# Where a weight conversion stands in a fused attention and two-MLP kernel, and which engines do it

## The chip, the cores and the metric

One core of a Trainium2 chip runs the whole program. The metric is the device time of one launch in microseconds (us), the median of several executions.

## What is computed

Windowed attention over 4 x 8 heads of 576 positions, a gated MLP with RMS norm, and a second MLP, all in single precision:

```python
scores = where(0 <= i - j < 64, q @ k.T / 8, -1e9)      # 4 batches, 8 heads, 576 x 64
x  = softmax(scores) @ v                                # 2304 tokens x 512
xn = x / sqrt(mean(x * x) + 1e-6) * rms_g
y  = (silu(xn @ w_gate) * (xn @ w_val)) @ w_out         # 512 -> 1536 -> 512
h  = y @ w_in                                           # 512 -> 2048
out = (h * sigmoid(1.702 * h)) @ w_out2                 # 2048 -> 512
```

The five weight matrices arrive as 64-bit floats, q, k and v as 32-bit floats.

## The kernel before

Every product is done in two parts: an operand is split into a rounded high part and the rest, and three of the four part products are summed. Tokens come in six blocks of 384, feature columns in chunks of 128.

The first half of the gated MLP (`for j in range(NB)`, blocks j = 0 to 5) runs beside the attention of the next block: for each chunk f, `proj` makes the gate and the value in PSUM tiles `psg` and `psv`, and `emit_O` adds the product with `w_out`. At the border of two blocks the next x is scaled (`rms_sum`, `rms_spread`, with a power on GpSimd at L439) and split into `xh` and `xl` (L462 to L466).

The second half (`for sb in range(NSB)`, `for p in range(NP1)`: nine pairs, called pair 0 to 8 here) takes two blocks and two chunks at a time by a scheme of seven products in place of eight. `chain(wg, ...)` makes the four gates and `chain(wv, ...)` the four values. A chain runs seven products of six matmuls into two PSUM tiles, `psa` and `psb`; between them ScalarE copies `psa` out (`snap`, L677) and VectorE adds `psb` to the copy (`plus`, L681). The product after next may not start until its tile has been read. `take` hands each result on: `gated` applies Silu (L853), `valued` multiplies and splits (L863 to L865). `fill` puts the matmuls of `half_groups` of the pair before between the products. TensorE's order is pinned to the program's from block 1 on. On the other engines the compiler orders the instructions by a simulated timeline in which the program's order is the priority, and it lets a ready instruction of low priority run where the engine looks idle. The third part (h chunks, f = 0 to 7 for three pairs of blocks) is built of the same chains.

A weight is turned from 64-bit to 32-bit floats in the kernel, 34 pairs of chunks in `w_order`, called c0 to c33 here. `w_step` does one of them and the second step of the one before it. The two ScalarE instructions (L201 scales the high words, L202 the low words) are kept behind `hold[0]`, the latest gate. VectorE then shifts the high words (L203), puts the sign bit back (L204) and adds the low words as integers (L207). `w_half` starts the next call: `w_products` (for gate, value and `w_in` chunks from c9 on) makes four block differences (L149 to L152), rounds seven blocks on ScalarE (`whi`, L157), makes the rest on VectorE (`wlo`, L158), and stores both to DRAM (L160, L161), from where `t_load` brings them back for each pair. For other chunks L175 and L176 do the same without differences. `w_load` issues the next raw weights on SP (L138). Tiles of tag "st" (raw words and converted words `m`) have 3 buffers, those of tag "w" 11.

c0 to c8 are converted in block 0, c9 to c17 in blocks 1 to 5, c18 to c25 (the `w_in` chunks) in the second half, where each pair of chunks calls `w_step(n_wi)` before its first chain:

```python
                if last:
                    nxo, left = x_first(raws)
                w_step(n_wi)
                a4 = {}
                ...
                chain(wg, xo, lambda i: groups[i - 2]() if i >= 2 else None, gated, nothing)
                ...
                groups = half_groups(sb, p, g, wo)
                wg, wv, wo = nwg, nwv, nwo
```

c26 to c33 (the last matrix) follow at the end of the second half and in the first eight chunks of the third part.

Of the kernel before, what the change touches and what calls it, by code (L numbers as in the profile page):

```python
# [8 lines left out]
F32 = mybir.dt.float32  # L9
F32R = mybir.dt.float32r  # L10
I32 = mybir.dt.int32
U32 = mybir.dt.uint32
AF = mybir.ActivationFunctionType
ALU = mybir.AluOpType
# [8 lines left out]
def window_attention__gated_mlp__mlp_kernel(  # L23
# [13 lines left out]
    nc = tc.nc  # L37
# [53 lines left out]
    def on_pe(op, *args, **kw):  # L91
        ins = op(*args, **kw)  # L92
        if pinned[0]:
            tc.keep_in_program_order(ins)
        return ins
# [16 lines left out]
    n_wh = len(w_order)  # L112
# [4 lines left out]
    n_wi = len(w_order)  # L117
    w_order += [(("p", p), ("p", p + NP2)) for p in range(NP2)]
    n_w = len(w_order)
    w_next = [0, 0]  # L120
# [20 lines left out]
    def after(ins):  # L141
        return tc.issue_after(ins) if ins is not None else nullcontext()
# [3 lines left out]
    def w_products(key, m):  # L146
        b11, b21, b12, b22 = (m[:, i * 256:(i + 1) * 256] for i in range(4))
        t = mt[0][:, 1, :].bitcast(F32).rearrange("p (b c) -> p b c", c=256)
        nc.vector.tensor_tensor(t[:, 0, :], b12, b11, ALU.subtract)  # L149
        nc.vector.tensor_tensor(t[:, 1, :], b22, t[:, 0, :], ALU.subtract)  # L150
        nc.vector.tensor_tensor(t[:, 2, :], b22, b12, ALU.subtract)
        nc.vector.tensor_tensor(t[:, 3, :], b21, t[:, 1, :], ALU.subtract)  # L152
        hi = wp.tile([128, 7, 256], F32R, tag="w", name="whi")
        lo = wp.tile([128, 7, 256], F32R, tag="w", name="wlo")
        for dst, src in ((slice(0, 2), m[:, 0:512]), (slice(2, 3), m[:, 768:1024]), (slice(3, 7), t)):
            src = src if src is t else src.rearrange("p (b c) -> p b c", c=256)
            nc.scalar.copy(hi[:, dst, :], src)  # L157
            nc.vector.tensor_tensor(lo[:, dst, :], src, hi[:, dst, :].bitcast(F32), ALU.subtract)  # L158
        d = dram.tile([128, 2, 7, 256], F32, name="w%s_%d" % key, tag="w%s_%d" % key)
        nc.sync.dma_start(out=d[:, 0], in_=hi.bitcast(F32))  # L160
        nc.sync.dma_start(out=d[:, 1], in_=lo.bitcast(F32))  # L161
        wd[key] = d
# [3 lines left out]
    def w_half():  # L166
        if not half:
            return
        pair, w24 = half.pop()
        kind, p = pair[0]  # L170
        paired = kind == pair[1][0] and p + 1 != pair[1][1]
        if paired and kind in "gvh":
            return w_products(pair[0], w24.bitcast(F32))
        w = wp.tile([128, 2, 1024], F32R, tag="w", name="w")
        nc.scalar.copy(w[:, 0, :], w24.bitcast(F32))  # L175
        nc.vector.tensor_tensor(w[:, 1, :], w24.bitcast(F32), w[:, 0, :].bitcast(F32), ALU.subtract)  # L176
        if paired:
            d = dram.tile([128, 2, 1024], F32, name=f"w{kind}_{p}", tag=f"w{kind}_{p}")
            nc.sync.dma_start(out=d, in_=w.bitcast(F32))
            wd[kind, p] = d  # L180
            weights[kind, p] = w
            return
        for e, key in enumerate(pair):
            weights[key] = w[:, :, e * 512:(e + 1) * 512]

    def w_step(limit):
        w_half()
        if w_next[1] >= min(limit, n_w):
            return
        w_load(w_next[1] + 1)  # L190
        pair = w_order[w_next[1]]
        w_next[1] += 1
        st = staged.pop(0).rearrange("p e (f two) -> p (e f) two", two=2)
        lo, hi = st[:, :, 0], st[:, :, 1]
        if w_next[1] <= n_wh:
            m = wp.tile([128, 1024], I32, tag="w", name="m")
        else:
            mt[0] = stp.tile([128, 2, 1024], I32, tag="st", name="m")
            m = mt[0][:, 0, :]
        with after(hold[0]):  # L200
            nc.scalar.mul(hi.bitcast(F32), hi.bitcast(F32), 2.0 ** -112)  # L201
            nc.scalar.activation(lo, lo.bitcast(U32), AF.Copy, scale=2.0 ** -29)  # L202
        nc.vector.tensor_scalar(m.bitcast(U32), hi.bitcast(U32), 3, None, ALU.logical_shift_left)  # L203
        nc.vector.scalar_tensor_tensor(  # L204
            m.bitcast(U32), hi.bitcast(U32), 0x80000000, m.bitcast(U32), ALU.bitwise_and, ALU.bitwise_or
        )
        nc.vector.tensor_tensor(m, m, lo, ALU.add)  # L207
        half.append((pair, m))
        w_load(w_next[1] + 2)

# [313 lines left out]
    for i in range(m0):  # L524
        m = m0 + i
# [15 lines left out]
    for m in range(2 * m0, N_ATT):  # L541
        b, i = divmod(m, m0)
        t, n = score_at[m - 2 * m0], score_at[m - 2 * m0 + 1] - score_at[m - 2 * m0]
# [13 lines left out]
    if True:  # L557
# [246 lines left out]
        def half_groups(sb, p, g, wo):  # L804
            if p == 0:
                banks = [(acc_p, f"acc{c}") for c in range(4)] + [(atp, "att")] * 2
                accs = [pool.tile([128, 512], F32, tag=tag, name="acc") for pool, tag in banks]
                spots[sb] = [(accs[c], accs[4 + c // 2][:, (c % 2) * 256:(c % 2 + 1) * 256]) for c in range(KC)]
            todo = [(e, c, pi, k) for e in (1, 0) for c in range(KC) for pi in range(3) for k in range(2)]

            def group(lo):
                for e, c, pi, k in todo[lo:lo + 12]:
                    first = p == 0 and e == 1 and pi == 0
                    shared = k == 1 and c % 2 == 1
                    on_pe(
                        nc.tensor.matmul,
                        spots[sb][c][k],
                        wo[:, (0, 1, 0)[pi], e * 512 + c * 128:e * 512 + (c + 1) * 128],
                        g[e][:, (0, 0, 1)[pi], slice(*PIECES[k])],
                        start=first and not shared,  # L820
                        stop=(p == NP1 - 1 and e == 0 and pi == 2),
                        skip_group_check=(k == 1),
                    )
                if p == NP1 - 1 and lo == 36:
                    for c in range(KC):
                        part = osp.tile([128, 2 * TB], F32, tag="os", name="part")
                        nc.sync.dma_start(out=part, in_=osd[sb][:, c, :])
                        for k in range(2):
                            sl = part[:, slice(*PIECES[k])]
                            nc.vector.tensor_tensor(sl, sl, spots[sb][c][k], ALU.add)  # L830
                        nc.sync.dma_start(out=x2d[sb][:, c, :], in_=part)

            return [lambda lo=lo: group(lo) for lo in (0, 12, 24, 36)]

        spots = {}
        for sb in range(NSB):
            last_sb = sb + 1 == NSB
            for p in range(NP1):
                last = p + 1 == NP1
                more = not (last and last_sb)  # L840
                nxt = 0 if last else p + 1
                if more:
                    nwg = t_load(("g", FH + nxt))
                if p == 1:
                    raws = x_raws((lambda e: x2d[0][:, :, e * TB:(e + 1) * TB]) if last_sb else (lambda e: xd[2 * sb + 2 + e]))
                if last:
                    nxo, left = x_first(raws)
                w_step(n_wi)
                a4 = {}

                def gated(q, c):
                    a4[q] = small("a" if q in (0, 3) else "ah")
                    hold[0] = nc.scalar.activation(a4[q], c, AF.Silu).ins  # L853

                chain(wg, xo, lambda i: groups[i - 2]() if i >= 2 else None, gated, nothing)
                if more:
                    nwv, nwo = t_load(("v", FH + nxt)), o_load(("o", FH + nxt))
                g = [xp.tile([128, 2, 2 * TB], F32R, tag="x", name="g") for _ in range(2)]

                def valued(q, c):  # L860
                    e, t = q % 2, q // 2
                    sl = slice(t * TB, (t + 1) * TB)
                    nc.vector.tensor_tensor(a4[q], a4[q], c, ALU.mult)  # L863
                    nc.scalar.copy(g[e][:, 0, sl], a4[q])
                    nc.vector.tensor_tensor(g[e][:, 1, sl], a4[q], g[e][:, 0, sl].bitcast(F32), ALU.subtract)  # L865

                chain(
                    wv, xo, lambda i: groups[i]() if i >= 2 else None, valued,
                    (lambda i: x_next(nxo, left)) if last else nothing,
                )  # L870
                groups = half_groups(sb, p, g, wo)
                wg, wv, wo = nwg, nwv, nwo
            xo = nxo

# [104 lines left out]
```

## Time and profile before

| | us |
|---|---|
| median of 3 runs | 983.26 (982.88 to 983.51) |
| the profiled execution, whole | 981.57 |
| its span on the core | 979.8 |
| TensorE busy in the span | 937.7 |
| VectorE / ScalarE / GpSimd busy | 571.8 / 495.0 / 12.2 |

The profile shows one execution. A row of a timeline gives the start in us from the start of the span, the duration, the engine, the line, the operation with the tiles written and read, and in brackets how long the engine stood idle before and what ended that. A line of groups gives busy time and mean duration. The median of the runs is 1.69 us above the profiled execution.

### The profile page before, as it was taken

How to read it: one execution, taken by the hardware profiler on the slowest of the kernel's cores; microseconds unless marked ns; L12 is line 12 of the kernel's file. 1: busy time of each engine (PE TensorE's matmuls, PEld its weight loads, DVE VectorE, ACT ScalarE, POOL GpSimd, SP SyncE). 2: the span in 40 equal slices, each digit the busy share in tenths (PEclk: the TensorE clock that was granted, in tenths of full speed). 3: DMA queues.
4: the chain of work that ended last, by engine and by line, in shares of the span. 5: the costliest groups of instructions: out<-in, count | busy, mean ns of one | idle time of the engine just before them, and what ended most of it. 6: DMA issues, size and time to landing. Idle time of an engine off the chain costs nothing.

```text
span 979.8 us, 15502 instructions
## 1 busy us (share of the span) xinstructions
PE 937.7 (96%) x5966; PEld 859.7 (88%) x5966; DVE 571.8 (58%) x1207; ACT 495.0 (51%) x1054; POOL 12.2 (1%) x39
## 2 busy tenths in 40 slices
PE   8889999999999897999999989999999999999998
PEld 7789898989989897988988979888888888888887
DVE  5898578577776875677777676645452223422222
ACT  7786566556564344464464365545543333523332
POOL 2000000000000000000000000000000000000000
PEclk9899899999999899999999999999999999999999
DMA  9956376746655589899999898776583535554301
GB/s 223 255 161 175 109 194 179 218 121 194 193 162 186 187 329 412 325 398 385 359 371 352 337 382 316 264 269 246 193 315 139 233 135 220 209 210 172 151 1 65
DMA packets 136074, 228.95 MB, mean 234 GB/s; under 512 B 79936, under 2 KB 106560, under 8 KB 131392
## 3 DMA queue, kind: packets, MB, share of 16 engines
q1 hardware_dynamic: 135472, 227.96, 66.8%
q8 instruction: 47, 0.77, 0.3%
q14 instruction: 27, 0.22, 0.1%
q10 hardware_dynamic: 528, 0.00, 0.0%
HBM read 171.84 MB, written 56.10 MB: 233 GB/s over the span
## 4 chain that ended last, share of the span: by engine, by line
PE 78%; DVE 8%; DMA 5%; ACT 5%; issue 2%; SPq 2%; POOL 0%; ACTq 0%; DVEq 0%
PE acc L92 32%; PE psa L92 16%; PE psb L92 12%; PE psg L92 6%; PE psv L92 6%; DMA wt<-wv 2%; PE ps_v L92 2%; ACT st L201 1%; SPq L266 1%; PE ps_s L92 1%; ACT st L202 1%; DMA st<-in_moe_w_val_dram 1%; PE ps_t L92 1%; DMA wo<-wo 1%; PE ps_r L92 1%
## 5 line engine op out<-in xcount | busy, mean ns | idle before, releaser
L92 PE MATMUL psa<-xop,wt 128*128 128x384 f32 x1008 | 206.2, 340 | 8.2 <-ACT al L677 6.5
L92 PEld LDWEIGHTS psa<-xop,wt 128*128 128x128 f32 x1008 | 177.6, 188 | 17.3 <-ACT al L677 9.1
L92 PE MATMUL psb<-xop,wt 128*128 128x384 f32 x756 | 155.0, 340 | 6.6 <-DVE al L681 5.1
L92 PEld LDWEIGHTS psb<-xop,wt 128*128 128x128 f32 x756 | 134.5, 188 | 13.7 <-DVE al L681 7.5
L92 PE MATMUL acc<-wo,g 128*128 128x512 f32 x576 | 144.4, 397 | 0.0
L92 PEld LDWEIGHTS acc<-wo,g 128*128 128x128 f32 x576 | 107.7, 188 | 21.1
L681 DVE TENSOR_TENSOR al<-al,psb 128x384 f32<-128x384 f32 x84 | 46.4, 553 | 123.0 <-PE psb L92 118.3
L938 DVE TENSOR_TENSOR g<-a,g 128x384 fp32r<-128x384 f32 x96 | 53.1, 556 | 58.7 <-ACT g L937 58.7
L92 PE MATMUL acc<-g,wo 128*128 128x512 f32 (+1 forms) x432 | 81.8, 337 | 0.3 <-DVE g L865 0.3
L92 PE MATMUL psg<-xh,w 128*128 128x384 f32 x288 | 69.5, 366 | 7.0 <-DVE xh L462 3.4
L92 PEld LDWEIGHTS acc<-g,wo 128*128 128x128 f32 x432 | 68.1, 188 | 8.6 <-DVE g L865 0.6
L92 PE MATMUL acc<-w,g 128*128 128x512 f32 x288 | 72.3, 397 | 0.0
L677 ACT COPY al<-psa 128x384 f32<-128x384 f32 x84 | 39.9, 475 | 53.6 <-PE psa L92 53.5
L681 DVE TENSOR_TENSOR s<-s,psb 128x384 f32<-128x384 f32 x42 | 23.2, 552 | 72.2 <-ACT s L677 72.2
L677 ACT COPY s<-psa 128x384 f32<-128x384 f32 x42 | 20.1, 479 | 86.6 <-PE psa L92 86.6
L92 PEld LDWEIGHTS acc<-w,g 128*128 128x128 f32 x288 | 53.9, 188 | 10.4
L92 PE MATMUL psv<-xh,w 128*128 128x384 f32 x288 | 62.3, 349 | 0.0
L92 PEld LDWEIGHTS psg<-xh,w 128*128 128x128 f32 x288 | 51.5, 197 | 11.2 <-DVE xh L462 4.9
L92 PE MATMUL acc<-ah,w 128*128 128x384 f32 x288 | 60.0, 344 | 0.0
L362 ACT ACTIVATE p<-p,sm 128x128 f32<-128x128 f32 x128 | 49.6, 394 | 17.0 <-DVE sm L350 17.0
L936 ACT ACTIVATE a<-al 128x384 f32<-128x384 f32 x48 | 25.2, 526 | 60.7 <-DVE al L681 59.3
L92 PEld LDWEIGHTS psv<-xh,w 128*128 128x128 f32 x288 | 52.1, 193 | 0.3 <-issue 0.2
(129 smaller groups left out, 1369.4 us busy)
## 6 DMA issues: line engine op xcount, KB each, us to landing
wt<-wh SPq DMA_DIRECT2D x48, 896.0 KB, 6.7
wo<-wp SPq DMA_DIRECT2D x16, 1024.0 KB, 4.7
wt<-wg SPq DMA_DIRECT2D x18, 896.0 KB, 10.8
wt<-wv SPq DMA_DIRECT2D x18, 896.0 KB, 8.9
st<-in_moe_w_out_dram SPq DMA_DIRECT2D x28, 512.0 KB, 4.4
xr<-x SPq DMA_DIRECT2D x12, 768.0 KB, 6.2
wo<-wo SPq DMA_DIRECT2D x9, 1024.0 KB, 10.4
st<-in_moe_w_in_dram SPq DMA_DIRECT2D x16, 512.0 KB, 6.9
```

What stands on the lines that cost most here:

```text
L92: ins = op(*args, **kw)
L201: nc.scalar.mul(hi.bitcast(F32), hi.bitcast(F32), 2.0 ** -112)
L202: nc.scalar.activation(lo, lo.bitcast(U32), AF.Copy, scale=2.0 ** -29)
L266: nc.sync.dma_start(out=t[off:off + n], in_=src[b, :, s:s + n, :].rearrange("h s d -> s h d"))
L362: last_exp[0] = nc.scalar.activation(p[e][:, hp, :], p[e][:, hp, :], AF.Exp, bias=sm[:, 0, i:i + 1], scale=-1.0, accum_out=sm[:, 1, i:i + ...
L677: nc.scalar.copy(t, a[:, :TB])
L681: nc.vector.tensor_tensor(t, t, b[:, :TB], ALU.add)
L936: hold[0] = nc.scalar.activation(a, c, AF.Gelu_apprx_sigmoid).ins
L938: nc.vector.tensor_tensor(g[1][:, q, :], a, g[0][:, q, :].bitcast(F32), ALU.subtract)
```

## The change

Three edits to the conversion. From c9 on, L201 becomes ScalarE's two-slope rectifier, which scales positive and negative words by different factors so that the sign ends in a bit that the shift of L203 moves to the top, and L204 falls away; the integer addition goes from VectorE to GpSimd. In all of `w_products`, the four differences go from VectorE to GpSimd. And in the second half `w_step` is called after the two chains of a pair and not before them.

```diff
     def w_products(key, m):
-        nc.vector.tensor_tensor(t[:, 0, :], b12, b11, ALU.subtract)
-        nc.vector.tensor_tensor(t[:, 1, :], b22, t[:, 0, :], ALU.subtract)
-        nc.vector.tensor_tensor(t[:, 2, :], b22, b12, ALU.subtract)
-        nc.vector.tensor_tensor(t[:, 3, :], b21, t[:, 1, :], ALU.subtract)
+        nc.gpsimd.tensor_tensor(t[:, 0, :], b12, b11, ALU.subtract)
+        nc.gpsimd.tensor_tensor(t[:, 1, :], b22, t[:, 0, :], ALU.subtract)
+        nc.gpsimd.tensor_tensor(t[:, 2, :], b22, b12, ALU.subtract)
+        nc.gpsimd.tensor_tensor(t[:, 3, :], b21, t[:, 1, :], ALU.subtract)
...
+        first = w_next[1] <= n_wh
         with after(hold[0]):
-            nc.scalar.mul(hi.bitcast(F32), hi.bitcast(F32), 2.0 ** -112)
+            if first:
+                nc.scalar.mul(hi.bitcast(F32), hi.bitcast(F32), 2.0 ** -112)
+            else:
+                nc.scalar.activation(hi.bitcast(F32), hi.bitcast(F32), AF.Prelu, scale=2.0 ** -112, alpha=-(2.0 ** 32))
             nc.scalar.activation(lo, lo.bitcast(U32), AF.Copy, scale=2.0 ** -29)
         nc.vector.tensor_scalar(m.bitcast(U32), hi.bitcast(U32), 3, None, ALU.logical_shift_left)
-        nc.vector.scalar_tensor_tensor(
-            m.bitcast(U32), hi.bitcast(U32), 0x80000000, m.bitcast(U32), ALU.bitwise_and, ALU.bitwise_or
-        )
-        nc.vector.tensor_tensor(m, m, lo, ALU.add)
+        if first:
+            nc.vector.scalar_tensor_tensor(
+                m.bitcast(U32), hi.bitcast(U32), 0x80000000, m.bitcast(U32), ALU.bitwise_and, ALU.bitwise_or
+            )
+        (nc.vector if first else nc.gpsimd).tensor_tensor(m, m, lo, ALU.add)
...
                     nxo, left = x_first(raws)
-                w_step(n_wi)
                 a4 = {}
...
                 groups = half_groups(sb, p, g, wo)
+                w_step(n_wi)
                 wg, wv, wo = nwg, nwv, nwo
```

## Rows read from the trace of the kernel before

**Rows 1.** The page: busy us, share of the span, instructions of each engine.
```profile
PE 937.7 (96%) x5966; PEld 859.7 (88%) x5966; DVE 571.8 (58%) x1207; ACT 495.0 (51%) x1054; POOL 12.2 (1%) x39
```
**Rows 2.** Busy time by stretch: PE, PEld, DVE, ACT, POOL, granted clock, DMA share, GB/s.
```profile
100.00:363.00 263.00, 251.65 (x2065) 237.66 (x2065) 188.55 (x499) 146.25 (x376) 3.40 (x4) 0.97 0.60 185
363.00:587.00 224.00, 210.10 (x1167) 195.22 (x1165) 159.73 (x263) 111.44 (x193) 0.00 (x0) 1.00 0.96 369
587.00:714.00 127.00, 126.95 (x637) 114.39 (x638) 70.25 (x102) 67.59 (x116) 0.00 (x0) 1.00 0.70 260
```
**Rows 3.** Waits of PE in 363 to 587: total us, times, longest.
```profile
PE psa L92 <- ACT al L677: 6.5, 8, 2.3
PE psb L92 <- DVE al L681: 5.1, 4, 1.6
```
**Rows 4.** Groups by line, whole span: count, busy us, mean ns, idle before.
```profile
L204 DVE SCALAR_TENSOR_TENSOR m<-st,m 128x1024 uint32<-128x1024 uint32 x34 | 41.6, 1223 | 0.6
L207 DVE CUSTOM_DVE_ANT_0 m<-st,m 128x2048 uint16<-128x2048 uint16 x34 | 41.5, 1222 | 0.7
...
L201 ACT ACTIVATE st<-st 128x1024 f32<-128x1024 f32 x34 | 38.7, 1137 | 3.4 <-DMA st<-in_moe_w_out_dram 1.7 <-DMA st<-in_moe_w_val_dram 1.7
L158 DVE TENSOR_TENSOR wlo<-m,whi 128x512 fp32r<-128x512 f32 (+2 forms) x42 | 31.4, 776 | 1.8 <-ACT whi L157 1.8
...
L149 DVE TENSOR_TENSOR m<-m 128x256 f32<-128x256 f32 x14 | 5.9, 421 | 0.1
...
L853 ACT ACT_TABLE_LOAD x1 | 1.3, 1283 | 0.0
...
L568 POOL MEMSET masks<- 128x768 f32 x1 | 0.7, 742 | 0.0
```
**Rows 5.** Timeline at the border of blocks 4 and 5.
```profile
318.92 1.22 DVE L207 CUSTOM_DVE_ANT_0 m<-st,m 128x2048 uint16<-128x2048 uint16 x1
...
321.80 2.01 PE L92 MATMUL psg<-xh,w 128*128 128x384 f32 x7 [2.17 <-DVE xh L462]
...
326.32 1.05 ACT L157 CAST whi<-m 128x1024 fp32r<-128x1024 f32 x1 [5.22 <-DVE m L152]
```
**Rows 6.** Timeline, pair 0, start of its second chain.
```profile
374.44 1.11 ACT L201 ACTIVATE st<-st 128x1024 f32<-128x1024 f32 x1
...
376.44 0.91 ACT L157 CAST whi<-m 128x512 fp32r<-128x512 f32 x2
...
377.77 1.33 PE L92 MATMUL psa<-xop,wt 128*128 128x384 f32 x6 [2.27 <-ACT al L677]
```
**Rows 7.** Timeline, pair 1, its first chain.
```profile
384.08 2.16 DVE L158 TENSOR_TENSOR wlo<-m,whi 128x512 fp32r<-128x512 f32 x3
...
386.75 1.33 PE L92 MATMUL psb<-xop,wt 128*128 128x384 f32 x6 [1.53 <-DVE al L681]
...
389.02 1.22 DVE L204 SCALAR_TENSOR_TENSOR m<-st,m 128x1024 uint32<-128x1024 uint32 x1
...
390.76 1.32 PE L92 MATMUL psb<-xop,wt 128*128 128x384 f32 x6 [1.62 <-DVE al L681]
```
**Rows 8.** Timeline, pairs 2 and 3: one conversion and its products.
```profile
415.30 1.23 DVE L207 CUSTOM_DVE_ANT_0 m<-st,m 128x2048 uint16<-128x2048 uint16 x1
416.56 1.22 SPq L138 DMA_DIRECT2D st<-in_moe_w_in_dram  x2
...
433.96 1.87 ACT L157 CAST whi<-m 128x512 fp32r<-128x512 f32 x3
```
**Rows 9.** Timeline, pair 8, its second chain.
```profile
572.75 1.32 PE L92 MATMUL psa<-xop,wt 128*128 128x384 f32 x6 [2.26 <-ACT al L677]
...
581.58 1.33 PE L92 MATMUL psb<-xop,wt 128*128 128x384 f32 x6 [1.55 <-DVE s L681]
```
**Rows 10.** Timeline, block 2: GpSimd's power beside a VectorE subtraction.
```profile
204.32 0.85 POOL L439 TENSOR_TENSOR ry<-rv,mhalf 128x3 f32<-128x3 f32 x1 [51.96 <-DVE rv L438]
...
204.58 0.56 DVE L755 TENSOR_TENSOR al<-a,ah 128x384 fp32r<-128x384 f32 x1 [0.34 <-ACT ah L754]
```

## The prediction

> **What bounds the kernel now.** I read the engines' line first: TensorE is busy for 937.7 of 979.8 us, VectorE for 58%, ScalarE for 51%, GpSimd for 1% [rows 1]. So a conversion costs nothing by its length; it costs only where it makes TensorE wait. Next come the stretches, to see where TensorE stands idle. In blocks 1 to 5 it is idle for 263.00 - 251.65 = 11.4 us, in the second half of the gated MLP for 224.00 - 210.10 = 13.9 us, in the first third of the last part, where c27 to c33 are converted, for 0.05 us [rows 2]. The nine conversions there can gain nothing. Then the waits of TensorE in the second half: nearly all end with the read of a PSUM tile, 6.5 us with ScalarE's copy of `psa` and 5.1 us with VectorE's addition of `psb` [rows 3]; two more kinds of the same sort make the rest. These two are short; they are late because something stands ahead of them in their queue. What stands there is read from the timelines [rows 5 to 7, 9], and the gain is the part of it that the change takes away.
>
> DMA is busy for 96% of that stretch [rows 2], but no wait of TensorE there ends with a landing [rows 3], so I take the loads as far enough ahead.
>
> **The change part by part.**
>
> *The sign.* L204 goes in 25 of 34 conversions: 25 x 1.223 = 30.6 us of VectorE [rows 4]. L201 becomes the rectifier. The trace has no rectifier. The nearest row is the scaling that it replaces, 1137 ns on the same shape [rows 4], and I take that. The other end is a reload of ScalarE's function table before and after it, 2 x 1283 ns [rows 4]; the trace has such loads only where the activation function changes, and copies and scalings run between the gates without one. Which kind the rectifier is, no row shows. The Trainium skill, "ScalarE: Activation LUTs", section "Table sets: the hidden batching unit", says that cheap functions such as relu and copy lie in every set; the two-slope form is not among those that it names.
>
> *The addition and the differences.* L207 leaves VectorE in 25 conversions, 25 x 1.222 = 30.6 us, and L149 to L152 in 14 products, 14 x 4 x 0.421 = 23.6 us [rows 4]. With the sign that makes 84.8 us less on VectorE: 571.8 becomes about 487. GpSimd takes them over. It has no such row. The lower end is its fill of 768 columns, 742 ns [rows 4], or about 1.0 us for 1024 columns and 0.25 for 256. The upper end is its power, 0.85 us for three columns [rows 10]; an addition at 0.28 us a column would take 290 us, and 25 of those would be 7 ms. I leave that end out of the range, because a power is many steps per element and an addition is one, as a fill is. I take twice VectorE's time, 2.4 us and 0.84 us: two inputs, on an engine whose fill runs at about one column per ns. GpSimd is then busy for 25 x 2.4 + 56 x 0.84 = 107 us more. In the second half this hides: from the end of an L207 at 416.53 to the rounding of its blocks at 433.96 are 17.4 us [rows 8], against 2.4 + 4 x 0.84 = 5.8 us. The Trainium skill, "GPSIMD Engine Reference", section "Performance versus the Vector engine", has 4497 ns for an addition of 2048 columns; an estimate from that page is 2.25 and 0.56 us, and the sum would not change by it.
>
> New waits: GpSimd's addition waits for L203 and L202, and behind it in GpSimd's queue stands the power of the next block border, once per block. ScalarE's L157 and VectorE's L158 wait for GpSimd where they waited for VectorE; behind L157 stand the copies of `psa` and the next gate. In blocks 1 to 5 ScalarE already stands 5.22 us before an L157 for the last difference [rows 5], because the differences are scattered through a full VectorE queue; on an empty GpSimd queue they should end sooner. SP's load of the next raw weights waits for the addition as it did (it is issued at 416.56, as L207 ends at 416.53 [rows 8]), with the loads for the chains behind it. L204 is gone ahead of it and the addition is longer by about as much: 0.
>
> *The move.* `w_step` goes from ahead of a pair's chains to behind them. But each conversion is tied to the latest gate, and what stands between the end of one pair and the start of the next is the same call. So I read the move as a shift by one pair: c18 is converted after the gates of pair 0 (where c19 is now, at 374.44 [rows 6]), c25 after those of pair 7, and c25's products come to pair 8, beside c26 and c27. Its SP work (two stores, two loads) goes along, behind the loads of values and `w_out` and ahead of the next gate load; those loads run a pair ahead, so I cost this at nothing. If that cover were gone, the price would be a late weight at each of nine chains.
>
> *What it does to the waits,* in the profiled execution:
> - Borders of blocks: at 321.80 TensorE has waited 2.17 us for `xh`, and L204 and L207 (2.44 us) stand ahead of it on VectorE [rows 5]. The addition of x parts there stays, so I count 2.0 us for this border and the earlier ones together; bounds 0 and 5.
> - Pair 0: 2.27 us, with two conversion instructions and 0.81 us of L157 (376.44 to 377.25) ahead of the copy [rows 6]. The conversion stays, by the shift; the products go a pair on. 0.7 us; bounds 0 and 2.27.
> - Pair 1: 1.53 and 1.62 us, with the rests of c18 (2.16 us) and the L203, L204 of c19 ahead of the addition of `psb` [rows 7]. c19 leaves this place, L204 is gone, the rests may stay. 2.4 us; bounds 0 and 3.15.
> - Pair 8: 2.26 us behind ScalarE, 1.55 us behind VectorE [rows 9]. VectorE loses two L204 and two L207 (4.9 us) and gets the three rests of c25 (2.16 us); ScalarE gets c25's three roundings, 1.87 us by the like of pair 3 [rows 8]. I take 0; bounds -1.5 and +2.
> - GpSimd beside VectorE (the second rival): I put +0.6 us for it; bounds 0 and +18.
>
> Sum: -2.0 - 0.7 - 2.4 + 0 + 0.6 = -4.5 us. Against the profiled execution, 981.57 - 4.5 = 977.1 us. The median of the runs is 1.69 us above it and should move with it: 983.26 - 4.5 = 978.8 us.
>
> **The rivals.** *Relief where nobody waits.* Most of the 84.8 us falls into stretches without a wait. If in the named places the rests, the additions of x parts and ScalarE's own work stay in front, the gaps stay too: a gain of 0 to 1.9 us, about 983 (981.3 to 985.2). For it speaks that the longest gaps, 2.27 and 2.26 us, end with ScalarE [rows 6, 9], which gains nothing.
>
> *Slower: GpSimd holds VectorE up.* For it: VectorE's splits read two SBUF tiles, and so do GpSimd's new instructions. Against it: the one place where the trace has both at once, L755 from 204.58, starts when ScalarE's cast releases it and takes 0.56 us, all of it inside GpSimd's power (204.32 to 205.17) [rows 10]; but the power reads three columns. The price: VectorE is busy for 159.73 of 224 us in the second half [rows 2], and I estimate about half of that as instructions with two SBUF inputs (L158, L628, L863, L865, against L681, L830 and the rest of the conversion); so about a third of 107 us, 36 us, would fall on each other. VectorE has the time; TensorE waits only if an addition of `psb` stands behind the held one. If every second microsecond of that reaches TensorE, it is +18 us, less the 5.1 gained: 983.26 + 12.9 = 996; at a quarter it is 987. It decides from 6 us on, a sixth of the overlap. The Trainium skill, "SBUF — State Buffer", section "Who interferes with whom", states it as a lock: GpSimd and a VectorE instruction with two SBUF inputs share a port pair, and whoever starts first keeps it for the whole instruction. By that rule this rival is the case; row 204.58 doesn't show it, for so short an operand.
>
> *The move does more.* If the conversions leave the place between the last gate and the first copy of `psa` altogether, the 2.27 and 2.26 us and the short gaps behind ScalarE (6.5 us in all [rows 3]) go too: 978.8 - 5 = 974.
>
> *Table reloads.* 25 x 2.57 = 64 us more of ScalarE. In the second half the place between gate and copy is full, so each of eight conversions would cost about 2.5 us, and as many at the borders: 983 + 20 to 40 us.
>
> **How the numbers follow.** Forecast 0.50 (978.8, own range 974 to 981.3); move does more 0.08; relief hidden 0.19; GpSimd holds VectorE 0.20 (985 to 996); reloads 0.03. The range leaves out the worst of the last two and the best of the second: 972.5 to 988. A measurement of this kernel can tell about 0.2%, 2 us, from no change. Faster: 0.58, from the first two. Same: 0.19. Slower: 0.23.
>
> **What would show it right or wrong.** VectorE's busy time falls to about 487 us; L204 and L207 have 9 instructions each left on VectorE; GpSimd is busy for about 120 us. The waits behind `psb` in pair 1 are gone or below 1 us, those in pair 0 still end with the copy of `psa`. ScalarE shows three table loads as before. The forecast is wrong if L158, L865 or L628 grow longer or start late while GpSimd works, if new waits stand behind L157, or if the gaps in pair 8 grow by more than 2 us.

## The result, and the profile after

The changed kernel takes 998.31 us (median of 4 runs, 994.28 to 998.65) against 983.07 us (981.91 to 983.51): 1.0147 times the time before, 95% interval 1.0120 to 1.0175. The forecast was 978.8 us, the range ended at 988. The profiled execution is the fastest of the four, 994.28 us with a span of 992.5.

The page's line of engines (busy us, share of the span, instructions), which answers to [rows 1]:

```profile
PE 942.5 (95%) x5966; PEld 861.5 (87%) x5966; DVE 554.2 (56%) x1101; ACT 496.2 (50%) x1054; POOL 131.2 (13%) x120
```

TensorE does the same 5966 matmuls. Its idle time rose from 979.8 - 937.7 = 42.1 to 992.5 - 942.5 = 50.0 us, and its busy time by 4.8 us for the same matmuls. VectorE fell by 17.6 us, not by the 84.8 of the prediction, which had it at about 487.

Busy time by stretch (as [rows 2]; the second stretch ends 3 us later, as the pairs do):

```profile
100.00:363.00 263.00, 247.80 (x2027) 231.88 (x2028) 179.49 (x451) 143.85 (x372) 47.45 (x37) 0.96 0.57 176
363.00:590.00 227.00, 210.55 (x1158) 195.87 (x1157) 144.04 (x202) 108.10 (x189) 56.70 (x41) 0.99 0.94 354
590.00:717.00 127.00, 125.65 (x636) 112.84 (x635) 70.91 (x95) 67.27 (x115) 18.28 (x7) 1.00 0.76 283
```

TensorE's idle time is 15.2, 16.4 and 1.35 us, where it was 11.4, 13.9 and 0.05: both stretches with waits got worse, and no stretch better. Both kernels run the same matmuls in the same order, so their places can be compared. Against the kernel before, the changed one is 6.5 us behind where that one is at 363 us, only 2.1 us at its 400 (the gaps of pairs 0 and 1 have shrunk) and 12.7 us at its 587; after that the distance stays. Waits of TensorE in the second half (total us, times, longest), as [rows 3]:

```profile
PE psa L92 <- ACT al L682: 6.3, 8, 1.5
PE psb L92 <- DVE al L686: 6.0, 5, 1.4
PE psb L92 <- DVE s L686: 3.2, 3, 1.5
```

They end with the same two readers as before, VectorE's one more often (8 times in place of 5). Why VectorE is late stands in its groups (by form: count, busy us, mean ns of one, idle before). First the kernel before, then the changed one, where line numbers are 4 or 5 higher:

```profile
L938 DVE TENSOR_TENSOR g<-a,g 128x384 fp32r<-128x384 f32 x96 | 53.1, 556 | 58.7 <-ACT g L937 58.7
L628 DVE TENSOR_TENSOR xop<-xr,xop 128x768 fp32r<-128x768 f32 x30 | 28.6, 955 | 16.2 <-ACT xop L627 16.0 <-DMA wt<-wh 0.2
L755 DVE TENSOR_TENSOR al<-a,ah 128x384 fp32r<-128x384 f32 x36 | 20.0, 555 | 8.5 <-ACT ah L754 8.5
L863 DVE TENSOR_TENSOR a<-a,al 128x384 f32<-128x384 f32 x9 | 5.0, 556 | 0.2
L462 DVE CAST xh<-xraw 128x384 fp32r<-128x384 f32 x12 | 3.9, 353 | 0.0
```

```profile
L943 DVE TENSOR_TENSOR g<-a,g 128x384 fp32r<-128x384 f32 x96 | 63.1, 659 | 60.0 <-ACT g L942 60.0
L686 DVE TENSOR_TENSOR al<-al,psb 128x384 f32<-128x384 f32 x84 | 46.4, 552 | 125.3 <-PE psb L92 122.4 <-ACT al L682 2.9
L633 DVE TENSOR_TENSOR xop<-xr,xop 128x768 fp32r<-128x768 f32 x30 | 39.3, 1315 | 12.5 <-ACT xop L632 12.4
L760 DVE TENSOR_TENSOR al<-a,ah 128x384 fp32r<-128x384 f32 x36 | 27.7, 769 | 13.0 <-ACT ah L759 13.0
L867 DVE TENSOR_TENSOR a<-a,al 128x384 f32<-128x384 f32 x9 | 12.2, 1357 | 0.1
L467 DVE CAST xh<-xraw 128x384 fp32r<-128x384 f32 x12 | 7.1, 617 | 0.0
```

The same instructions on the same shapes got longer, up to 2.4 times in the mean, and only where an operand pair lies in SBUF; the exception is the cast L467 with a single input. L686, which reads one operand from PSUM, kept its 0.55 us. Summed over VectorE's rows that lie beside a GpSimd row (each less the median of its own form alone), 57.7 us were added; I call this the *held time* below. GpSimd's groups:

```profile
L212 POOL TENSOR_TENSOR m<-m,st 128x1024 int32<-128x1024 int32 x25 | 62.2, 2489 | 420.1 <-ACT st L206 297.4 <-DVE m L207 42.6 <-DMA qkv<-in_q_dram 27.4
L149 POOL TENSOR_TENSOR m<-m 128x256 f32<-128x256 f32 x14 | 14.9, 1063 | 1.1
```

One such place in the timeline (start, duration, engine, line, idle before), and how it reaches TensorE:

```profile
503.23 1.13 ACT L206 ACTIVATE st<-st 128x1024 int32<-128x1024 uint32 x1
504.49 2.42 POOL L212 TENSOR_TENSOR m<-m,st 128x1024 int32<-128x1024 int32 x1 [17.45 <-ACT st L206]
505.11 2.61 DVE L633 TENSOR_TENSOR xop<-xr,xop 128x768 fp32r<-128x768 f32 x1 [1.05 <-ACT xop L632]
507.65 0.54 DVE L686 TENSOR_TENSOR al<-al,psb 128x384 f32<-128x384 f32 x1
508.24 2.29 PE L92 MATMUL psb<-xop,wt 128*128 128x384 f32 x6 [1.41 <-DVE al L686]
```

GpSimd's addition starts 0.13 us after ScalarE's L206 (503.23 + 1.13 = 504.36). VectorE's L633 starts inside it and ends at 507.72, 0.81 us after the addition's end at 506.91, though alone it takes 0.95. L686 stands behind it, and TensorE waits 1.41 us for that. Then its six matmuls take 2.29 us in place of 1.33 [rows 7], because the granted clock falls (columns as in [rows 2]):

```profile
505.00:508.00 3.00, 1.32 (x6) 1.00 (x6) 2.89 (x2) 2.32 (x5) 2.92 (x2) 1.00 1.00 421
508.00:512.00 4.00, 3.76 (x13) 3.76 (x14) 4.00 (x5) 1.32 (x3) 3.92 (x4) 0.57 1.02 328
```

TensorE had been busy for 1.32 of 3 us; then the mean granted clock was 0.57, so mostly 1.2 GHz and not 2.4. At this place the held instruction is paid for twice. It is the only such place in the second half of this profile; behind the other waits there the six matmuls take 1.31 to 1.33 us.

### The profile page after: what moved, and what is told of

It is laid out like the page before. It is cut to its first block, busy times and chain, and to the rows that moved or that the text cites. A ratio compares the mean times of both kernels' runs of the same rounds, so it can differ in the third digit from the quotient of the medians.

```text
span 992.5 us, 15545 instructions
## 1 busy us (share of the span) xinstructions
PE 942.5 (95%) x5966; PEld 861.5 (87%) x5966; DVE 554.2 (56%) x1101; ACT 496.2 (50%) x1054; POOL 131.2 (13%) x120
## 4 chain that ended last, share of the span: by engine, by line
PE 76%; issue 10%; DVE 8%; ACT 5%; POOL 1%; DMA 0%; ACTq 0%; DVEq 0%; POOLq 0%
PE acc L92 30%; PE psa L92 15%; PE psb L92 12%; PE psg L92 6%; PE psv L92 6%; PE ps_v L92 2%; PE ps_s L92 1%; ACT st L205 1%; DVE xop L633 1%; PE ps_t L92 1%; PE ps_r L92 1%; ACT st L206 1%; DVE al L686 1%; ACT quad L367 1%; PE ps_k L92 1%
## 5 line engine op out<-in xcount | busy, mean ns | idle before, releaser
L92 PEld LDWEIGHTS psb<-xop,wt 128*128 128x128 f32 x756 | 135.4, 189 | 16.4 <-DVE al L686 7.9
L212 POOL TENSOR_TENSOR m<-m,st 128x1024 int32<-128x1024 int32 x25 | 62.2, 2489 | 420.1 <-ACT st L206 297.4
L686 DVE TENSOR_TENSOR al<-al,psb 128x384 f32<-128x384 f32 x84 | 46.4, 552 | 125.3 <-PE psb L92 122.4
L943 DVE TENSOR_TENSOR g<-a,g 128x384 fp32r<-128x384 f32 x96 | 63.1, 659 | 60.0 <-ACT g L942 60.0
L92 PE MATMUL psg<-xh,w 128*128 128x384 f32 x288 | 71.9, 373 | 9.0 <-DVE xh L467 6.5
L686 DVE TENSOR_TENSOR s<-s,psb 128x384 f32<-128x384 f32 x42 | 23.2, 551 | 86.4 <-ACT s L682 86.4
L92 PEld LDWEIGHTS psg<-xh,w 128*128 128x128 f32 x288 | 52.4, 201 | 14.6 <-DVE xh L467 9.2
```

The costliest lines, as they stand in the source:

```text
L212: (nc.vector if first else nc.gpsimd).tensor_tensor(m, m, lo, ALU.add)
L686: nc.vector.tensor_tensor(t, t, b[:, :TB], ALU.add)
L943: nc.vector.tensor_tensor(g[1][:, q, :], a, g[0][:, q, :].bitcast(F32), ALU.subtract)
```

## The experiments

*Holding theory:* a VectorE instruction with two SBUF inputs and a GpSimd instruction exclude each other for the whole instruction, and TensorE waits behind the held one. *Rivals:* the lateness of GpSimd's slower results; a loss from the rectifier or the move; a cost of the place. Each ratio is to the kernel before in the same series; "held" is worked out as above, from one profile.

| kernel | median us | ratio (95%) | held us | GpSimd busy us |
|---|---|---|---|---|
| changed kernel | 998.31 | 1.0147 (1.0120 to 1.0175) | 57.7 | 131.2 |
| sign edit alone | 985.02 | 1.0024 (1.0011 to 1.0036) | 0 | 12.1 |
| move alone | 981.16 | 0.9982 (0.9971 to 0.9993) | 0 | 12.1 |
| sign and move | 985.03 | 1.0024 (1.0014 to 1.0034) | 0 | 12.1 |
| additions alone on GpSimd | 991.43 | 1.0089 (1.0069 to 1.0108) | 15.2 | 77.1 |
| differences and `x_split` on GpSimd | 1016.64 | 1.0337 (1.0308 to 1.0366) | 42.6 | 148.5 |
| differences alone on GpSimd | 989.36 | 1.0066 (1.0038 to 1.0094) | 7.4 | 62.4 |
| changed, GpSimd's operands cut | 973.02 | 0.9890 (0.9860 to 0.9921) | 0 | 32.9 |
| changed, GpSimd's work in pieces | 996.64 | 1.0135 (1.0111 to 1.0159) | 27.3 | 196.9 |
| additions of c26 to c33 on GpSimd | 983.86 | 1.0008 (0.9995 to 1.0022) | 5.7 | 32.8 |
| GpSimd for c9 to c17 only | 991.00 | 1.0077 (1.0058 to 1.0096) | 20.9 | 56.2 |
| GpSimd from c18 only (mirror image) | 992.99 | 1.0097 (1.0072 to 1.0121) | 35.3 | 87.0 |
| mirror image, placed | 980.69 | 0.9975 (0.9964 to 0.9985) | 13.6 | 79.0 |
| the same place, all on VectorE | 981.71 | 0.9982 (0.9974 to 0.9991) | 0 | 12.1 |
| mirror image, all on VectorE | 983.79 | 1.0007 (0.9998 to 1.0016) | 0 | 12.2 |

**The edits one by one.** The sign edit alone, the addition left on VectorE:

```diff
+            if first:
+                nc.scalar.mul(hi.bitcast(F32), hi.bitcast(F32), 2.0 ** -112)
+            else:
+                nc.scalar.activation(hi.bitcast(F32), hi.bitcast(F32), AF.Prelu, scale=2.0 ** -112, alpha=-(2.0 ** 32))
...
+        if first:
             nc.vector.scalar_tensor_tensor(
...
```

> Only the sign edit: from c9 on the rectifier stands in for the scaling and the or-step on VectorE falls away; addition and differences stay on VectorE, the call stays ahead of the chains. Hold theory (GpSimd's two-input instructions keep VectorE's instructions with two SBUF inputs waiting): nothing of the loss is here; VectorE's busy time falls by 25 x 1.22 = 31 us to about 541, and the time is 978 to 983 us. Order theory (the loss comes from the new instruction order that any lighter VectorE queue brings): some of the loss shows, 986 us or more. Table theory: three table loads if the rectifier lies in every function set, over 50 and 1000 us or more if not.

985.02 us: 0.24% slower, though VectorE's busy time falls to 543.5 us. That lies between the figures of the holding and the order theory; the table loads stay three. In the profile most of the loss comes at one place, the border of blocks 2 and 3. The timeline of the kernel before:

```profile
217.18 0.28 DVE L350 CUSTOM_DVE_ANT_0 p<-ps_s,masks 128x128 f32<-128x128 f32 x1
...
218.21 1.15 PE L92 MATMUL ps_v<-pt,qkv 128*64 128x64 f32 x32 [1.97 <-issue]
...
219.81 0.69 DVE L158 TENSOR_TENSOR wlo<-m,whi 128x512 fp32r<-128x512 f32 x1
```

The same place with the sign edit alone:

```profile
216.57 0.42 DVE L158 TENSOR_TENSOR wlo<-m,whi 128x256 fp32r<-128x256 f32 x1
216.91 0.28 DVE L355 CUSTOM_DVE_ANT_0 p<-ps_s,masks 128x128 f32<-128x128 f32 x1
...
217.93 1.98 PE L92 MATMUL ps_v<-pt,qkv 128*64 128x64 f32 x32 [3.10 <-issue]
```

The stretch around it (columns as in [rows 2]), before:

```profile
216.00:223.50 7.50, 5.53 (x61) 5.19 (x60) 7.50 (x31) 5.66 (x21) 0.00 (x0) 1.00 0.69 213
```

and with the sign edit alone:

```profile
216.00:223.50 7.50, 5.57 (x45) 5.38 (x46) 6.92 (x27) 5.24 (x19) 0.00 (x0) 0.55 0.49 122
```

With an L204 gone ahead of them, the rests L158 go in front of the softmax steps; before, they came behind. TensorE waits 1.1 us longer; the profile names no releaser ("issue"), but in both kernels the wait ends 1.0 us after the first softmax step (L350, then L355) starts. The mean granted clock is 0.55 there in place of 1.00, and the position of the same matmuls slips by 3.5 us across this place. The kernel with sign and move slips there by the same 3.5 us. Relief on VectorE is not neutral where it changes the order.

The move alone:

```diff
-                w_step(n_wi)
                 a4 = {}
...
                 groups = half_groups(sb, p, g, wo)
+                w_step(n_wi)
```

> Only the move of the call behind the two chains. Shift theory (prediction): every conversion of the second half sits after the same gate one pair later, pair 1 loses its gaps, pair 8 gets the products of c25: 980 to 984 us. Order theory: the move by itself makes the second half 4 to 8 us longer, about 990 us. Hold theory alone: no loss here.

981.16 us, -0.18%, as the shift theory had it. The waits of pair 1 are gone and pair 0's is 1.52 us.

Sign and move together, all of GpSimd's new work back on VectorE (against the changed kernel; so with all four differences):

```diff
-        nc.gpsimd.tensor_tensor(t[:, 0, :], b12, b11, ALU.subtract)
+        nc.vector.tensor_tensor(t[:, 0, :], b12, b11, ALU.subtract)
...
-        (nc.vector if first else nc.gpsimd).tensor_tensor(m, m, lo, ALU.add)
+        nc.vector.tensor_tensor(m, m, lo, ALU.add)
```

> The changed kernel with the addition and the differences back on VectorE; sign edit and move stay. Hold theory: the whole loss goes, 975 to 982 us, and VectorE's instructions with two SBUF inputs (L943 or its like) are back at about 0.56 us. Order theory: still above 988 us.

985.03 us, between the two theories' figures again: each had a part of the loss. Without GpSimd the change is 0.24% slower, and GpSimd's work makes the rest: 1.0147 - 1.0024, or 12 us.

**GpSimd's two parts.** The kernel before with one edit:

```diff
-        nc.vector.tensor_tensor(m, m, lo, ALU.add)
+        (nc.vector if first else nc.gpsimd).tensor_tensor(m, m, lo, ALU.add)
```

> Only the integer addition of c9 to c33 on GpSimd, all else as before (the or-step and the differences on VectorE, the call ahead of the chains). Hold theory: 25 additions of about 2.5 us, each holding whatever two-input instruction VectorE meets, so VectorE shows instructions of over 2 us and the time is 4 to 10 us above before, 987 to 993. Order theory: within 2 us of before.

991.43 us. The splits L628 and L755 (their line numbers are one higher there) rise to 1.09 and 0.75 us in the mean.

Then the differences on GpSimd (the first of four, and a line of `x_split` that came along unintended):

```diff
-        nc.vector.tensor_tensor(t[:, 0, :], b12, b11, ALU.subtract)
+        nc.gpsimd.tensor_tensor(t[:, 0, :], b12, b11, ALU.subtract)
...
-            nc.vector.tensor_tensor(t[:, 1], src, t[:, 0].bitcast(F32), ALU.subtract)
+            nc.gpsimd.tensor_tensor(t[:, 1], src, t[:, 0].bitcast(F32), ALU.subtract)
```

> Only the four block differences of c9 to c25 on GpSimd, all else as before. Hold theory: 56 instructions of about 1 us instead of 25 of 2.5 us; a held VectorE instruction then takes up to 1.5 us, and the loss is smaller than with the addition (which gave 991.4): 984 to 988 us. Order theory: no relation to GpSimd's durations, within 2 us of before.

1016.64 us. The edit was wider than this text says: besides the four differences it had also moved the subtraction of `x_split` (L628, 42 instructions) to GpSimd. It says nothing of the differences by themselves, so they were taken alone (the same diff without the line of `x_split`):

> The kernel before with the four block differences of w_products (L149 to L152) on GpSimd and nothing else; x_split stays on VectorE. Holding theory (a VectorE instruction with two SBUF inputs and a GpSimd instruction exclude each other for the whole instruction): 56 differences of about 1.05 us, 59 us of GpSimd, of which a third to a half falls on VectorE instructions of that kind, 10 to 25 us of holding in VectorE's rows; 985 to 991 us, each held instruction by at most about 1.1 us. Rival, delivery only (GpSimd is just slower per difference, 1.05 us against 0.42): no VectorE row longer than in the kernel before; 983 to 985 us, and gaps only behind L157.

989.36 us, within the holding theory's figure, but with 7.4 us of held time where 10 to 25 were expected. Its timeline at the border of blocks 1 and 2 shows another way to lose:

```profile
159.61 4.33 POOL L149 TENSOR_TENSOR m<-m 128x256 f32<-128x256 f32 x1 [6.92 <-DVE m L207]
...
163.90 0.73 POOL L151 TENSOR_TENSOR m<-m 128x256 f32<-128x256 f32 x1
...
166.16 1.04 ACT L157 CAST whi<-m 128x1024 fp32r<-128x1024 f32 x1 [5.46 <-POOL m L152]
167.24 1.23 DVE L158 TENSOR_TENSOR wlo<-m,whi 128x1024 fp32r<-128x1024 f32 x1 [3.89 <-ACT whi L157]
...
169.41 1.66 PE L92 MATMUL ps_v<-pt,qkv 128*64 128x64 f32 x32 [3.98 <-issue]
```

Here VectorE holds GpSimd: a run of splits leaves a difference of 0.73 us no place, and it takes 4.33. L157 waits for the last difference, L158 for L157, and the softmax stands behind L158 in VectorE's order, so TensorE waits 3.98 us. Holding and lateness are not two rivals but one chain. The profile is that of this kernel's slowest execution (994.40 us), so I take from it the mechanism and not the size.

**Without its length.** The changed kernel with GpSimd's operands cut to 4 columns (the roundings read the converted words instead):

```diff
-            (nc.vector if first else nc.gpsimd).tensor_tensor(m, m, lo, ALU.add)
+            nc.gpsimd.tensor_tensor(m[:, 0:4], m[:, 0:4], lo[:, 0:4], ALU.add)
...
-        nc.gpsimd.tensor_tensor(t[:, 0, :], b12, b11, ALU.subtract)
+        nc.gpsimd.tensor_tensor(t4[:, 0, :], b12[:, 0:4], b11[:, 0:4], ALU.subtract)
```

> The changed kernel with every GpSimd addition and difference cut to 4 columns: the rest of the addition and of the differences is left out, the roundings read the converted words instead. The number of GpSimd instructions and their waits stay. Hold theory: with GpSimd done in a fraction of a us nothing is held, VectorE's L943 is back at 0.56 us and the time is that of the kernel with everything on VectorE or below, 976 to 986 us. Wait theory (the new waits on another engine's queue are what costs): still above 990.

973.02 us, 25 us below the changed kernel and below the range of either theory, with no instruction held. This also takes the waits for GpSimd's results away, so the 25 us are the price of both. It is 13 us below sign and move too (1.0024 - 0.9890), where the same work stays on VectorE: leaving the work out was worth that much, and having GpSimd do it in full cost about twice as much.

**In pieces.** The same work as 8 additions of 128 columns and 2 differences of 128:

```diff
+            for i in range(8):
+                c = slice(i * 128, (i + 1) * 128)
+                nc.gpsimd.tensor_tensor(m[:, c], m[:, c], lo[:, c], ALU.add)
```

> The changed kernel with the same GpSimd work in shorter instructions: eight additions of 128 columns for one of 1024, two differences of 128 for one of 256. Hold by the instruction: a VectorE instruction is held for one piece at most, about 0.5 us, so the longest L943 falls from 2.57 to about 1.1 us and the time to 985 to 992 us although GpSimd is busy for longer. Hold for as long as GpSimd has work queued: L943 stays at 2.5 us or grows and the time stays at 995 to 1000.

996.64 us: hardly better. The rows fit the first theory, for the longest split `g<-a,g` takes 0.83 us in place of 2.57; the time fits the second, for another reason. The held time halves, to 27.3 us, but GpSimd needs 196.9 us (an addition of 128 columns takes 0.64 us, eight of them 5.1 against 2.49), and the lateness grows:

```profile
570.35 1.05 ACT L159 CAST whi<-m 128x1024 fp32r<-128x1024 f32 x1 [3.79 <-POOL m L154]
571.30 0.47 ACT L689 COPY al<-psa 128x384 f32<-128x384 f32 x1
...
571.83 2.29 PE L92 MATMUL psa<-xop,wt 128*128 128x384 f32 x6 [6.63 <-ACT al L689]
```

**Where it costs.** The kernel before with additions on GpSimd only for the last matrix, c26 to c33:

```diff
-        nc.vector.tensor_tensor(m, m, lo, ALU.add)
+        (nc.vector if w_next[1] <= n_wi else nc.gpsimd).tensor_tensor(m, m, lo, ALU.add)
```

> The kernel before with the integer addition on GpSimd for c26 to c33 alone (end of the second half and third part). Hold theory: VectorE's split (L938 and its like) again shows single instructions of about 2.5 us, but TensorE has slack there (0.05 us idle in 127), so the time is that of before within 2 us. If a held VectorE instruction always costs, 8 x 2 us = 16 us: 995 or more.

983.86 us, no change, with 5.7 us of held time (one split takes 2.22 us): in the third part TensorE hardly waits at all ([rows 2], 0.05 us). Then GpSimd's work of the changed kernel only up to block 5 (first two lines), and only from c18 on, with the rectifier from c18 too (last two):

```diff
+        eng = nc.vector if key[0] == "h" else nc.gpsimd
+        (nc.vector if first or w_next[1] > n_w1 else nc.gpsimd).tensor_tensor(m, m, lo, ALU.add)
...
+        eng = nc.vector if key[0] != "h" else nc.gpsimd
+        first = w_next[1] <= n_w1
```

> The changed kernel with GpSimd's additions and differences kept for c9 to c17 only (blocks 1 to 5); from c18 on both are back on VectorE, with the rectifier and the move kept. Holding theory: the loss of the changed kernel up to the end of block 5 stays and the loss of the second half goes; against 985.0 for all on VectorE, 988 to 993 us. Rival, the holding costs only in the second half, where pairs leave VectorE less room: about 985 us. Held VectorE instructions appear before 363 us alone.

> The mirror image: rectifier, GpSimd's additions and differences from c18 on only, and the move; c9 to c17 are converted as in the kernel before. Holding theory: 986 to 992 us, with held VectorE instructions after 363 us alone; TensorE's time up to 363 us as in the kernel before. Rival, the holding costs only in blocks 1 to 5: 979 to 982 us.

991.00 and 992.99 us (the second 1 us above its range): it costs in both. Against the kernels without GpSimd, 1.0077 - 1.0024 and 1.0097 - 1.0007, it is 5.2 and 8.8 us, together 14.0; the changed kernel pays 12.

**The same work in another place.** The mirror image with VectorE's shift, on which the addition waits, put behind the last split of the second chain:

```diff
-        nc.vector.tensor_scalar(m.bitcast(U32), hi.bitcast(U32), 3, None, ALU.logical_shift_left)
+        with after(None if first else last_val[0]):
+            nc.vector.tensor_scalar(m.bitcast(U32), hi.bitcast(U32), 3, None, ALU.logical_shift_left)
```

> The same as the mirror image, with one thing more: VectorE's shift of the high words (L203), on which GpSimd's addition waits, comes behind the last split of the pair's second chain, so that GpSimd's addition and its differences run beside the next first chain, where VectorE has only additions with a PSUM input, as the prediction had assumed of the place. Holding theory: GpSimd's instructions are as many and as long, but hardly a VectorE instruction is held in the second half; 976 to 982 us, 5 to 14 us faster than the mirror image. Rival, GpSimd's mere length or lateness costs: as slow as the mirror image or slower, 986 to 995 us, with gaps behind L157 or late weights.

980.69 us, 12 us faster than the mirror image and faster than the kernel before. One addition in the mirror image, then in the placed kernel:

```profile
399.10 2.44 POOL L213 TENSOR_TENSOR m<-m,st 128x1024 int32<-128x1024 int32 x1 [14.27 <-ACT st L207]
399.94 2.00 DVE L868 TENSOR_TENSOR a<-a,al 128x384 f32<-128x384 f32 x1
```

```profile
411.83 2.46 POOL L214 TENSOR_TENSOR m<-m,st 128x1024 int32<-128x1024 int32 x1 [16.63 <-issue]
412.67 0.56 DVE L689 TENSOR_TENSOR al<-al,psb 128x384 f32<-128x384 f32 x1 [1.06 <-PE psb L92]
...
414.37 0.74 POOL L150 TENSOR_TENSOR m<-m 128x256 f32<-128x256 f32 x1
```

Beside the addition VectorE now has only the sum with `psb`, which is not held, and the difference takes 0.74 us. One of the eight conversions is still held (at 387.55 L644 takes 3.08 us in place of 0.95). The groups of the four differences have means of 0.78 to 0.94 us, in the mirror image 1.04 to 1.13. Of the 13.6 us of held time that are left, 9.8 lie in the third part, so 3.8 up to its start, where the mirror image has 23.6. Is it the place or GpSimd? The same place with all on VectorE, and the mirror image with all on VectorE:

> The kernel with GpSimd's work placed beside the next first chain, with its integer addition and its differences back on VectorE: the place of the shift, the rectifier from c18 on and the move are kept, GpSimd does nothing new. If the 12 us between the placed kernel (980.7 us) and its mirror image (993.0 us) came from GpSimd no longer holding VectorE up, this kernel lies within 3 us of the placed one, 978 to 983 us. If the place of the shift is worth a gain by itself, which GpSimd's work still ate a part of, it lies at 973 to 977 us. If GpSimd relieves VectorE in a way that TensorE feels, it lies at 984 to 988 us.

> The rectifier from c18 on and the move, everything on VectorE, the shift where the changed kernel has it; c9 to c17 are converted as in the kernel before. It is the mirror image (993.0 us) without GpSimd. Holding theory: GpSimd's 16 additions and 32 differences cost the mirror image what lies between it and this kernel; with the move's gain of 2 us (981.2 us for the move alone) and the rectifier's relief of the second half, 977 to 981 us, so that the price of GpSimd in the second half is 12 to 16 us. If the rectifier costs in the second half too, as it did in blocks 1 to 5 (985.0 us for the sign edit alone), it lies at 983 to 987 us.

981.71 and 983.79 us (in both the additions and `eng` are on VectorE throughout). GpSimd's same 16 additions and 32 differences cost 1.0097 - 1.0007 = 0.90% (8.8 us) in the one place and nothing measurable in the other (0.9975 against 0.9982, the intervals overlap). The place of the shift by itself is worth 0.25%.

The nothing is a sum of two parts, as the stretches show (columns as in [rows 2]), first of the placed kernel, then of the same place with all on VectorE:

```profile
363.00:587.00 224.00, 211.62 (x1169) 197.10 (x1168) 128.79 (x209) 111.84 (x194) 47.61 (x41) 0.99 0.93 353
587.00:600.00 13.00, 13.00 (x76) 12.14 (x75) 9.56 (x13) 8.19 (x13) 4.62 (x2) 1.00 0.90 323
```

```profile
363.00:587.00 224.00, 215.95 (x1202) 200.71 (x1201) 150.65 (x255) 113.38 (x196) 0.00 (x0) 1.00 0.95 364
587.00:600.00 13.00, 10.76 (x44) 9.44 (x43) 6.65 (x12) 6.89 (x11) 0.00 (x0) 0.74 1.00 376
```

In the second half TensorE is idle for 12.4 us in the placed kernel against 8.1 us, so GpSimd's work costs there even in the good place. The kernel on VectorE loses that again at the start of the third part: TensorE waits 2.24 us for an addition of `psb` behind two conversions, and the mean granted clock is 0.74. Each is one profile.

The second text expected 977 to 981 us from the rectifier's relief; that did not come, and its other figure did. In what way the rectifier costs from c18 on (0.25% more than the move alone) stays open: its profile is 1.9 us behind the kernel before already at 120 us, where both do the same work, and at 610 us TensorE waits 2.2 us for VectorE's `part` (L835), where the move alone waits 0.8 us.

## Why the prediction was wrong, step by step

**The step that failed** is the term "GpSimd beside VectorE", put at +0.6 us. GpSimd's work measured 12 us against the same work on VectorE, and 25 us against the kernel with its operands cut. The rival named for it was the right mechanism, and its 985 to 996 us was close, with a chance of 0.20. A sign that the prediction had named came: L628 grew from 0.955 to 1.315 us. Two readings led there:

- [Rows 10] were taken as evidence against holding. A power of three columns beside one subtraction shows nothing about an addition of 1024. In the changed kernel 60 rows beside a GpSimd row are over a fifth longer than their form alone. The rule of the Trainium skill that the prediction set against it ("SBUF — State Buffer", section "Who interferes with whom": a lock on a shared port pair, kept for the whole instruction by whoever starts first) agrees with the rows at 504.49 and 505.11: 2.61 us in place of 0.95. It also exempts VectorE instructions with at most one SBUF input, as L686 at 0.55 us shows, unless they run in a two-port mode; that would cover the held cast L467 (0.88 us beside GpSimd, 0.35 alone), but no row shows its mode.
- The cover was costed by length and not by place. "This hides", because 17.4 us lay between the end of L207 and the rounding of its blocks [rows 8]. In the kernel before, the integer addition waited in VectorE's full queue: in pairs 0 to 6 it starts 14.6 to 17.1 us after L202. On the empty GpSimd queue it starts 0.13 us after (504.49 above), beside the second chain's splits. Nobody needed the result earlier; it only moved into a bad place. The placed kernel undoes just this.

The rival's price was also built wrongly on both sides: it took 36 us of overlap, half of it reaching TensorE. It was 57.7 us of held time and 12 us of loss, about a fifth; the loss holds lateness and VectorE's relief as well.

**The rest of the sum**, -5.1 us, measured +2.4 us in sign and move. That kernel keeps the additions and differences on VectorE, which the sum had taken away, so the 12 us above are already less their relief. With all of it off VectorE and GpSimd's operands cut, the gain is about 11 us (0.9890): the sum had the relief too small and its price far too small.

- *The sign.* The rectifier takes 1.131 us (forecast 1.137), and ScalarE has three table loads as before: right. Taking L204 away was to gain 2.0 us at the borders; it cost, through the order at 217 us. At the border of blocks 4 and 5 the wait for `xh` [rows 5] is 1.7 us without GpSimd; with it, it is 3.85 us, behind two held L633 (4.02 us) and a held L760.
- *The move* as a shift by one pair was right: pair 0 fell from 2.27 us [rows 6] to 1.50, forecast 0.7 less; in pair 1 both waits [rows 7] are gone. The rows of the changed kernel:

```profile
383.52 1.32 PE L92 MATMUL psa<-xop,wt 128*128 128x384 f32 x6 [1.50 <-ACT al L682]
387.53 1.33 PE L92 MATMUL psa<-xop,wt 128*128 128x384 f32 x6 [0.57 <-ACT s L682]
```

  Alone it brought 1.8 of the 3.1 us: new waits of about 1 us each behind the copy of `psa` come in three later pairs.
- *GpSimd's own time.* 2.49 us per addition (forecast 2.4) and 1.03 per difference (0.84; alone 0.73, the rest is VectorE holding it): 119 us more, forecast 107.
- *VectorE's relief.* The 84.8 us added up durations, but rows partly overlap: in the kernel with cut operands, where nothing is held, VectorE falls by 71.5 us (to 500.3). In the changed kernel the held time takes most of that back.

Counted from sign and move, the two misses, 7.5 and 11.5 us, make 19.0 of the 19.5 us between forecast and median.

## What to carry to other kernels

Before work goes from VectorE to GpSimd, list VectorE's instructions with two SBUF inputs in the stretch where the moved work will run, and ask which of them TensorE waits behind; the relief on VectorE's busy time is a gain only as far as TensorE waited behind it, and here the holding cost more than that. An empty queue starts work the moment its input is there, so give moved work a place by hand: the same GpSimd instructions cost 9 us beside the splits and, all told, nothing measurable beside sums that read PSUM. Cutting them into pieces only traded holding for lateness.

## What the runs showed of the hardware

The exclusion goes both ways and holds per instruction. In the third part of the changed kernel the second to start waits for the first:

```profile
631.15 2.43 POOL L212 TENSOR_TENSOR m<-m,st 128x1024 int32<-128x1024 int32 x1 [12.89 <-ACT st L206]
631.45 2.55 DVE L943 TENSOR_TENSOR g<-a,g 128x384 fp32r<-128x384 f32 x1 [0.73 <-ACT g L942]
...
678.99 0.56 DVE L943 TENSOR_TENSOR g<-a,g 128x384 fp32r<-128x384 f32 x1 [0.73 <-ACT g L942]
679.00 2.85 POOL L212 TENSOR_TENSOR m<-m,st 128x1024 int32<-128x1024 int32 x1 [13.70 <-ACT g L942]
```

By the records, at 631 GpSimd is first and VectorE's 0.56 us become 2.55; at 679 VectorE is first by 0.01 us, keeps its 0.56, and the addition takes 2.85. A run of VectorE instructions can keep GpSimd out for longer still (4.33 us for 0.73 above).
